# Block attention and a two-layer network: an order planned at build time, and seven products in place of eight for 32 of 36 tiles

## The chip, the cores and the metric

The kernel runs on one core of a Trainium2 chip. A core has five engines, each with its own queue of instructions that it runs strictly in order: TensorE (PE in the profile) multiplies matrices, VectorE (DVE) and ScalarE (ACT) work on elements, GpSimd (POOL) copies and issues loads, SyncE (SP) issues transfers. Sixteen DMA engines move data. Engines wait for each other through semaphores. TensorE writes into PSUM, eight banks of 2 KB per partition; the other data lie in SBUF, 128 partitions.

The metric is the time of one execution on the device, in microseconds (us). The kernel before has a median of 286.15 us over 3 runs (285.52 to 287.26).

## The reference

Inputs are q, k and v of 8 batches, 8 heads, 576 positions and 64 elements per head, and two weights. Attention is computed inside chunks of 64 positions only, so each chunk sees itself alone; its result is the input of a two-layer network without biases.

```python
scores = scale * np.matmul(q_c, k_c.transpose(0, 1, 2, 4, 3))    # chunks of 64
scores = scores - np.max(scores, axis=-1, keepdims=True)
attn = np.exp(scores)
attn = attn / (np.sum(attn, axis=-1, keepdims=True) + 1e-09)
out = np.matmul(attn, v_c)
...
x = np.ascontiguousarray(attn_out.transpose(0, 2, 1, 3)).reshape(B * S, H * D)
...
h = x @ w_in                      # 4608 x 512 by 512 x 2048
g = np.maximum(0.01 * h, h)
return (g @ w_out).astype(np.float32)     # 4608 x 2048 by 2048 x 512
```

Inputs and output are float32; the kernel multiplies in float16.

## The kernel before, in words

The 4608 tokens are 36 tiles of 128 tokens, two chunks each.

**Attention of a tile**, by stages that each stand in one function (lines 539 to 675). q and k are loaded as float16 by GpSimd (`load_qk`, line 64; float32 in memory, cast on the way). For tiles 0 to 8 TensorE transposes them into PSUM (`stage_tq`, `stage_tk`) and VectorE or ScalarE copies them out (`stage_q`, `stage_k`); from tile 9 on SP does it by DMA transposes (`stage_t`, line 563: QT and KT), and GpSimd spreads QT into QZ, a block-diagonal form (`stage_p`, line 571). Then: 8 products into the bank Sp (`stage_s`, line 578), the maximum mx and the shift sh on VectorE, the exponential ex on ScalarE, the sum z, its reciprocal zi and the norm en on VectorE, a transpose into et (`stage_e` and `stage_c` on TensorE and VectorE up to tile 8, `stage_d`, line 642, by SP's DMA from tile 9 on), 8 products with v into xp (`stage_v`, line 651), and ScalarE's copy into xT (`stage_a`, line 669), a ring of 1536 tokens. v lies in VB, two batches, loaded by `load_v`. The buffers for q and k hold 9 tiles.

**The first layer** takes blocks of tokens (`BLOCKS`, line 45: six of 128, three of 256, six of 512). `mm1` fills one bank hT with 512 columns: 4 hidden groups of 128 tokens, 2 of 256 or one of 512, by `SUB`. ScalarE applies the leaky ReLU into gT (`act1`).

**The second layer** is plain for the first 9 blocks (`PLAIN`, 12 tiles): `mm2`, 16 products of 512 columns for each 128 tokens into oP. For the other six blocks (24 tiles) it is Strassen's scheme: the block of g and w_out are cut into 2 x 2 parts, and 7 products take the place of 8 (`product`, line 273, banks ma, mb, mc). It needs sums of weight parts (`weight_form`, WF, five once), sums of parts of g (`form`, S1, S2, S5 and two in place, five a block) and combinations of results (`evict` on ScalarE, `combine` on VectorE, `piece` in the last block), before SP stores them.

**What sets the order.** Emission order is each engine's order. The loads go out first, by the string `LOADS` (line 118). The first five tiles follow a list written by hand (`FRONT`, line 724), in which `i12` stands for 12 idle products that keep TensorE at work while it waits. Then a loop (line 756) makes one round for each tile: Sp and the softmax of one tile, the q and k of another, xp of a third, and six units of the two layers, which `pick` takes from a list by costs kept in `T` and `when`. Loads run 7 tiles ahead of the round, transposes of q and k 3 ahead. A tile's xp comes two rounds after its Sp.

Of the kernel before, what the change touches and what calls it, by code (L numbers as in the profile page):

```python
# [12 lines left out]
AXL = mybir.AxisListType  # L13


@with_exitstack
def kernel(
# [31 lines left out]
    HB, HM = NFC // 2, d_model // 2  # L49

# [3 lines left out]

# [7 lines left out]
    qk: dict[int, tuple[bass.AP, bass.AP]] = {}  # L62

    def load_qk(u):

        both = []
        for name, src in (("q_in", q), ("k_in", k)):
            t = sbp.tile([128, H, D], FP16, name=name, tag=name, bufs=NIN)
            r0, r1 = u * G, (u + 1) * G
            cut = min(-(-r0 // S) * S, r1) if r0 % S else r1  # L70
            for a, z in ((r0, cut), (cut, r1)):
                if a < z:
                    nc.gpsimd.dma_start(  # L73
                        out=t[a - r0:z - r0],
                        in_=src[a // S, :, a % S:a % S + z - a, :].rearrange("h p d -> p h d"),
                    )
            both.append(t)
        qk[u] = tuple(both)

    def load_v(b):  # L80
        for m in range(2):
            nc.gpsimd.dma_start(  # L82
                out=VB[b % NVB][m * CH:(m + 1) * CH, :, :, m * CH:(m + 1) * CH].rearrange("p h c d -> p (h c) d"),
                in_=v[b, m * H // 2:(m + 1) * H // 2].rearrange("h (c j) d -> j (h c) d", j=CH),
            )

    def load_w_in(f0, f1):
        for m in range(2):
# [5 lines left out]
    def load_w_in_quarter(a):  # L94
        load_w_in(512 * a, 512 * a + 512)

    def load_w_out_quarter(a):
        load_w_out(4 * a, 4 * a + 4)

    def load_w_out(f0, f1):  # L100
        nc.gpsimd.dma_start(
            out=w_outT[:, f0:f1, :],
            in_=moe_w_out[f0 * 128:f1 * 128, :].rearrange("(fb p) m -> p fb m", p=128),
        )

    first = []
    for eng, name, src in ((nc.sync, "q_f", q), (nc.scalar, "k_f", k)):
        t = sbp.tile([128, H, D], FP32, name=name, tag=name, bufs=1)
        eng.dma_start(out=t, in_=src[0, :, 0:G, :].rearrange("h p d -> p h d"))
        first.append(t)  # L110
    one = sbp.tile([128, 1], FP16, name="one")
    nc.vector.memset(one, 0.0)
    nc.scalar.activation(out=one, in_=one, func=AFT.Exp, bias=0.0, scale=1.0)
    zeros = sbp.tile([128, 1], FP16, name="zeros")
    nc.vector.memset(zeros, 0.0)
    qk[0] = tuple(sbp.tile([128, H, D], FP16, name=n, tag=n, bufs=NIN) for n in ("q_in", "k_in"))

    LOADS = (
        "g1 v0 g2 Q0 Q1 g3 Q2 Q3 g4 P0 P1 P2 P3 g5 v1 g6 g7 g8 "
    )  # L120
    LOADERS = {"g": load_qk, "v": load_v, "Q": load_w_in_quarter, "P": load_w_out_quarter}
    ident = sbp.tile([128, 128], FP16, name="ident")
    for n, what in enumerate(LOADS.split()):
        LOADERS[what[0]](int(what[1:]))
        if n == 0:
            make_identity(nc, ident)

    gT: dict[int, bass.AP] = {}
    GT: dict[int, tuple[int, bass.AP]] = {}

    def tile_of(j):

        return 0 if j < 4 else 1 if j < 6 else 2 if j < 8 else j - 5

    START = [sum(BLOCKS[:j]) for j in range(len(BLOCKS))]
    mm_n = {"n": 0, "of": 4}

    def mm_tile(shape, name):

        i = mm_n["n"] % mm_n["of"]  # L140
        mm_n["n"] += 1
        return psp.tile(shape, FP32, name=name, tag=f"mm{i}", bufs=1)


    T = {"pe": 0.0, "dve": 0.0, "act": 0.0}

    def on(engine, us, after=0.0):
        T[engine] = max(T[engine], after) + us
        return T[engine]

    UNIT = 0.87
    when: dict[tuple, float] = {}

    HT: dict[tuple[int, int, int], bass.AP] = {}
    parts: dict[tuple[int, int], int] = {}
    oP: dict[tuple[int, int], bass.AP] = {}
    made: dict[int, int] = {}
    read = {"tokens": 0}

    def sub(j):  # L160
        return SUB.get(j, BLOCKS[j])

    def mm1(j, a, h=0):
        tb = sub(j)
        r0 = START[j] + h * tb
        nf = 512 // tb
        hT = mm_tile([128, nf, tb], "hT")
        for i in range(nf):
            fc = nf * a + i
            for t in range(NT):  # L170
                nc.tensor.matmul(  # L171
                    out=hT[:, i, :],
                    lhsT=w_inT[:, t, fc * 128:(fc + 1) * 128],
                    rhs=xT[:, t, r0 % RING:r0 % RING + tb],
                    start=(t == 0),
                    stop=(t == NT - 1),
                )
        on("pe", UNIT)
        HT[j, a, h] = hT
        made[j] = made.get(j, 0) + 1  # L180
        if made[j] == NFC * BLOCKS[j] // 512:
            read["tokens"] = START[j] + BLOCKS[j]

    def act1(j, a, h=0):
        tb = sub(j)
        nf = 512 // tb
        n = tile_of(j)
        if n not in GT:
            GT[n] = START[j], sbp.tile([128, NFC, 512], FP16, name="gT", tag="gT", bufs=2)
        gT[j] = GT[n][1][:, :, START[j] - GT[n][0]:START[j] - GT[n][0] + BLOCKS[j]]  # L190
        nc.scalar.activation(  # L191
            out=gT[j][:, nf * a:nf * a + nf, h * tb:h * tb + tb], in_=HT.pop((j, a, h)),
            func=AFT.Prelu, bias=0.0, scale=1.0, alpha=0.01,
        )
        when["gT", j] = on("act", 0.62, T["pe"] + 0.2)

    def mm2(j, ti, part):
        n = parts.get((j, ti), 0)
        if n == 0:
            oP[j, ti] = mm_tile([128, d_model], "oP")  # L200
        o = oP[j, ti]
        for fc in range(part * 4, part * 4 + 4):
            nc.tensor.matmul(  # L203
                out=o,
                lhsT=gT[j][:, fc, ti * 128:(ti + 1) * 128],
                rhs=w_outT[:, fc, :],
                start=(n == 0 and fc == part * 4),
                stop=(n == NFC // 4 - 1 and fc == part * 4 + 3),
            )
        on("pe", UNIT)  # L210
        parts[j, ti] = n + 1

    def store(j, ti):
# [3 lines left out]
        r0 = START[j] + ti * 128  # L217
        nc.sync.dma_start(out=out[r0:r0 + 128, :], in_=osb)

# [249 lines left out]
    def pick():  # L469
# [5 lines left out]
        if not can:  # L475
            return None
# [347 lines left out]
```

## Time and profile before

| | us |
|---|---|
| median of 3 runs | 286.15 |
| fastest, slowest run | 285.52, 287.26 |
| span of the profiled execution | 285.7 |
| TensorE busy | 275.5 |
| VectorE busy | 193.8 |
| ScalarE busy | 149.4 |
| GpSimd busy | 128.1 |

The profile gives the span, from the first instruction to the last, as the profiled execution's time; it is 0.45 us below the median of the runs, which were timed apart from it. A busy time is the union of an engine's instructions. A line such as "L298 PE MATMUL mb<-WF,gT ... x8" names the source line, the engine, what is written and what is read, and how many instructions are merged; the numbers ahead are the start and the duration in us. A unit's last products are drawn past the next unit's start, because matrix products are pipelined: the pace is read from one start to the next. In brackets stands the idle time ahead of a group and what ended it. "DMA to landing" is the time from the issue of a transfer to its semaphore.

### The profile page before, as it was taken

How to read it: one execution, taken by the hardware profiler on the slowest of the kernel's cores; microseconds unless marked ns; L12 is line 12 of the kernel's file. 1: busy time of each engine (PE TensorE's matmuls, PEld its weight loads, DVE VectorE, ACT ScalarE, POOL GpSimd, SP SyncE). 2: the span in 40 equal slices, each digit the busy share in tenths (PEclk: the TensorE clock that was granted, in tenths of full speed). 3: DMA queues.
4: the chain of work that ended last, by engine and by line, in shares of the span. 5: the costliest groups of instructions: out<-in, count | busy, mean ns of one | idle time of the engine just before them, and what ended most of it. 6: DMA issues, size and time to landing. Idle time of an engine off the chain costs nothing.

```text
span 285.7 us, 7255 instructions
## 1 busy us (share of the span) xinstructions
PE 275.5 (96%) x3012; PEld 226.3 (79%) x3012; DVE 193.8 (68%) x322; ACT 149.4 (52%) x264; POOL 128.1 (45%) x166
## 2 busy tenths in 40 slices
PE   4979999999999999999999999999999999999995
PEld 4969855877949585899989899998999998666784
DVE  6987515666687776557888888888888840820392
ACT  6347733655738374777356546554565554535320
POOL 8846646876585647657538495332410000000000
PEclk9999999999999999999999999999999999999999
DMA  9999999999999999999999999999714301200213
GB/s 131 170 189 179 192 165 195 143 180 162 175 147 173 158 156 184 162 157 134 155 154 158 139 188 197 153 136 249 114 30 112 93 2 73 76 0 0 110 59 129
DMA packets 165825, 39.14 MB, mean 137 GB/s; under 512 B 156832, under 2 KB 161440, under 8 KB 165792
## 3 DMA queue, kind: packets, MB, share of 16 engines
q0 software_dynamic: 114336, 18.09, 91.5%
q1 hardware_dynamic: 50416, 20.33, 42.8%
q8 instruction: 23, 0.38, 0.5%
q10 hardware_dynamic: 1040, 0.26, 0.4%
q14 instruction: 10, 0.08, 0.1%
HBM read 36.70 MB, written 9.44 MB: 161 GB/s over the span
## 4 chain that ended last, share of the span: by engine, by line
PE 84%; DMA 6%; DVE 5%; ACT 2%; issue 1%; POOL 1%; ACTq 0%; POOLq 0%
PE hT L171 40%; PE oP L203 15%; PE mb L298 10%; PE mc L298 7%; PE ma L298 6%; DMA k_in<-in_k_dram 4%; PE xp L657 3%; PE Sp L583 2%; DMA VB<-in_v_dram 2%; DVE S L263 2%; ACT ex L605 1%; ACT gT L191 1%; DVE en L622 1%; PE kp L547 1%; DVE sh L598 0%
## 5 line engine op out<-in xcount | busy, mean ns | idle before, releaser
L171 PE MATMUL hT<-xT,w_inT 128*128 128x256 f16 (+2 forms) x1344 | 143.4, 257 | 1.9 <-DMA w_inT<-in_moe_w_in_dram 0.9
L171 PEld LDWEIGHTS <-w_inT 128*128 128x128 f16 x1344 | 107.6, 98 | 15.6 <-issue 2.6
L191 ACT ACTIVATE gT<-hT 128x512 f16<-128x512 f32 x144 | 85.5, 595 | 54.5 <-PE hT L171 53.3
L576 POOL COPY QZ<-QT 64x512 f16<-64x512 f16 x54 | 36.5, 676 | 53.0 <-DMA QT<-q_in 34.1
L203 PE MATMUL oP<-w_outT,gT 128*128 128x512 f16 x192 | 44.9, 379 | 0.0
L298 PEld LDWEIGHTS <-gT 128*128 128x128 f16 x384 | 37.5, 98 | 6.2
L605 ACT ACTIVATE ex<-sh 128x512 f16<-128x512 f32 x36 | 22.6, 627 | 33.7 <-DVE sh L598 33.6
L73 POOL DMA_DIRECT2D k_in<-in_k_dram x39 | 32.9, 845 | 15.9 <-DVE z L612 4.1
L612 DVE TENSOR_REDUCE z<-ex 128x8 f32<-128x512 f16 x36 | 24.7, 685 | 21.1 <-ACT ex L605 20.9
L593 DVE TENSOR_REDUCE mx<-Sp 128x8 f32<-128x512 f32 x36 | 24.7, 686 | 18.1 <-PE Sp L583 18.0
L73 POOL DMA_DIRECT2D q_in<-in_q_dram x39 | 33.2, 851 | 7.0 <-DMA w_outT<-in_moe_w_out_dram 2.4
L298 PEld LDWEIGHTS <-S 128*128 128x128 f16 x288 | 28.1, 98 | 5.0 <-DVE S L263 0.5
L203 PEld LDWEIGHTS <-gT 128*128 128x128 f16 x192 | 17.6, 98 | 17.7
L622 DVE TENSOR_TENSOR en<-ex,zi 128x512 f16<-128x512 f16 x36 | 27.2, 757 | 1.2
L673 ACT ACTIVATE xT<-xp 128x512 f16<-128x512 f32 x36 | 21.3, 592 | 9.4 <-PE xp L657 9.4
L598 DVE TENSOR_TENSOR sh<-Sp,mx 128x512 f32<-128x512 f32 x36 | 24.9, 691 | 1.2
L298 PE MATMUL mb<-WF,gT 128*128 128x256 f16 x192 | 24.6, 273 | 0.0
L263 DVE TENSOR_TENSOR S<-gT 128x2048 f16<-128x2048 f16 x18 | 22.3, 1278 | 1.5 <-ACT gT L191 1.5
L82 POOL DMA_DIRECT2D VB<-in_v_dram x16 | 18.5, 1161 | 0.0
L215 ACT ACTIVATE osb<-oP 128x512 f32<-128x512 f32 x12 | 7.2, 597 | 18.4 <-PE oP L203 18.4
L657 PEld LDWEIGHTS <-VB 128*128 128x128 f16 x288 | 13.1, 98 | 3.1 <-issue 0.6
L583 PEld LDWEIGHTS <-QZ 128*128 128x128 f16 x288 | 13.2, 99 | 2.2 <-issue 0.3
(57 smaller groups left out, 233.2 us busy)
## 6 DMA issues: line engine op xcount, KB each, us to landing
out_dram<-osb SPq DMA_DIRECT2D x10, 512.0 KB, 3.5
VB<-in_v_dram POOLq DMA_DIRECT2D x16, 288.0 KB, 13.2
q_in<-in_q_dram POOLq DMA_DIRECT2D x31, 128.0 KB, 13.1
k_in<-in_k_dram POOLq DMA_DIRECT2D x31, 128.0 KB, 13.6
out_dram<-osb SPq DMA_DIRECT2D x14, 256.0 KB, 6.8
w_inT<-in_moe_w_in_dram POOLq DMA_DIRECT2D x8, 256.0 KB, 9.7
w_outT<-in_moe_w_out_dram POOLq DMA_DIRECT2D x4, 512.0 KB, 9.9
q_in<-in_q_dram POOLq DMA_DIRECT2D x8, 64.0 KB, 9.1
```

The costliest lines, as they stand in the source:

```text
L73: nc.gpsimd.dma_start(out=t[a - r0:z - r0], in_=src[a // S, :, a % S:a % S + z - a, :].rearrange("h p d -> p h d"),)
L171: nc.tensor.matmul(out=hT[:, i, :], lhsT=w_inT[:, t, fc * 128:(fc + 1) * 128], rhs=xT[:, t, r0 % RING:r0 % RING + tb], start=(t == 0), sto ...
L191: nc.scalar.activation(out=gT[j][:, nf * a:nf * a + nf, h * tb:h * tb + tb], in_=HT.pop((j, a, h)), func=AFT.Prelu, bias=0.0, scale=1.0, a ...
L203: nc.tensor.matmul(out=o, lhsT=gT[j][:, fc, ti * 128:(ti + 1) * 128], rhs=w_outT[:, fc, :], start=(n == 0 and fc == part * 4), stop=(n == ...
L263: nc.vector.tensor_tensor(out=to, in0=of, in1=by, op=op)
L298: nc.tensor.matmul(out=BANK[bank][:, p, :] if j < LAST else ENDS[bank, p], lhsT=lhs[:, fc, p * 128:(p + 1) * 128], rhs=rhs[:, fc, :], star ...
L576: nc.gpsimd.tensor_copy(out=QZ[u % NQZ][part, :, :, s, :], in_=qt[part])
L593: nc.vector.tensor_reduce(out=MX[u], in_=SP[u], axis=AXL.X, op=ALU.max)
L598: nc.vector.tensor_tensor(out=SH[u], in0=SP.pop(u), in1=MX.pop(u).unsqueeze(2).to_broadcast((128, 8, CH)), op=ALU.subtract)
L605: nc.scalar.activation(out=E[u], in_=SH.pop(u), func=AFT.Exp, bias=0.0, scale=SCL)
L612: nc.vector.tensor_reduce(out=z, in_=E[u], axis=AXL.X, op=ALU.add)
L622: nc.vector.tensor_tensor(out=E[u], in0=ex, in1=ZI.pop(u).unsqueeze(2).to_broadcast((128, 8, CH)), op=ALU.mult)
```

## The change

The loop, the hand-written list and the picking are replaced by a planner that runs while the program is built. Every step is a task with an engine (or a choice of engines), a duration, the tasks it depends on, a place in the wished order (`pos`), and for PSUM a bank that it takes and the tasks that free it. The planner keeps a clock for each engine and a model of the DMA queues, takes the task that can begin first, among those within `SLACK` the one with the smallest `pos`, and emits it. The resulting order is fixed in the program; nothing of the plan is present when it runs.

```diff
+class Planner:
+    LAG = 0.035
...
+    def advance(self, to):
+        for k, r in self.heads().items():
+            self.queues[k][0][1] -= r * (to - self.now)
+        self.now = to
+        for q in self.queues.values():
+            while q and q[0][1] <= 1e-9:
+                n, _, _, _, kind = q.pop(0)
+                lat = 1.5 if kind != "turn" else 3.2 if self.queues.get("sw") else 0.4
+                self.landings.append((to + lat, n))
...
-    BLOCKS = [128] * 6 + [256] * 3 + [512] * 6
-    PLAIN = 9
-    SUB = {7: 128, 9: 256, 10: 256, 11: 256, 12: 256, 13: 256}
+    BLOCKS = [128]*4+[256]*4+[512]*6
+    PLAIN = 4
+    SUBS = {}
+    LEAD = 3.49
+    LOADS = 'g1 v0.0 i v0.1 g2 Q0 Q2 g3 Q1 Q3 P0 g4 P2 P1 g5 g6 P3 v1.0 v1.1 g7 g8'
...
-        "g1 v0 g2 Q0 Q1 g3 Q2 Q3 g4 P0 P1 P2 P3 g5 v1 g6 g7 g8 "
...
+    plan = Planner(
+        {"mm": ["qp", "kp", "mm0", "mm1", "mm2", "mm3"], "Sp": ["Sp"], "ox": ["ox"]}, SLACK
+    )
...
+    def att(u, step=0.0):
+        return (first_pos(u - LEAD) + ATT + 0.001 * step if u >= 4 else -10 + u + 0.01 * step) + TWEAK.get((u, step), 0.0)
...
+            add(("e", u), {"SP": (1.3, 1.3)}, turn_e_dma(u), [("n", u), ("v", u - 4)], dma=("turn", 0.77, 0.024), pos=p(u, -5))
...
+        add(("v", u), {"PE": (0.233, 0.40)}, values(u), vd, pos=p(u, 12), bank="ox", frees=[("a", u)])
...
+    def fill(since, at):
+        tags = [(x, k) for k, x in plan.banks["mm"].items() if x is not None and x <= since]
+        n = int((at - since) * FILLS / 0.056) - 1
+        if since < FILL and tags and n > 1:
+            to = psum([128, 4, 128], FP32, "idle", min(tags)[1])
+            for i in range(n):
+                nc.tensor.matmul(out=to[:, i % 4, :], lhsT=ones, rhs=ones, start=True, stop=True)
...
+    plan.gap = fill
+    plan.run()
```

What differs in the work itself:

- Second layer: plain for 4 tiles instead of 12; seven products for four blocks of 256 tokens (4 to 7) and the six of 512. For a block of 256 the sums and results have half the width.
- First layer: units of 128 columns for 4 tiles instead of 8, all others of 256 columns; the 512-column units of the last block are gone.
- Loads: in `LOADS` g is a tile's q and k, v a batch's v, Q and P quarters of w_in and w_out, i the identity matrix. In the built order the first v stands behind tile 2; Q2 ahead of Q1, P0 ahead of tile 4, tile 6 and P3 ahead of the second v. Later loads stand where the planner put them, between GpSimd's copies.
- Idle products read a tile of ones instead of the identity, and are put where the plan leaves TensorE idle before 24 us: 175 instead of 120.
- The banks for seven-product results, first-layer units and transposes come from one pool of six.
- Up to tile 8 the copies of q and k go to VectorE or ScalarE, as the planner finds them free.
- In the built order, the last block's products begin before those of the block ahead of it are done: five units stand between the last first-layer unit and the first product that reads S2.

On TensorE the built order has 144 first-layer units (16 of 128 columns, 128 of 256), 16 plain second-layer units and 112 of the seven products; before it was 32, 96 and 16 (of 512), 48 and 84. The attention's pieces are the same in number.

More of the change, by code (lines that the diff above doesn't have):

```diff
@@ L80, in load_v @@
-    def load_v(b):
-        for m in range(2):
+    ident = sbp.tile([128, 128], FP16, name="ident")
+    one = sbp.tile([128, 1], FP16, name="one")
+    ones = sbp.tile([128, 128], FP16, name="ones")
+    zeros = sbp.tile([128, 1], FP16, name="zeros")
+    plan = Planner(
+        {"mm": ["qp", "kp", "mm0", "mm1", "mm2", "mm3"], "Sp": ["Sp"], "ox": ["ox"]}, SLACK
+    )
+    add = plan.add
+    copy = {"DVE": (0.40, 0.46), "ACT": (0.52, 0.62), "POOL": (0.61, 0.66)}
+    dve = {"DVE": (0.69, 0.72)}
@@ new lines, with either, block_of, first_pos @@
+    act = {"ACT": (0.53, 0.62)}
+    def either(eng, out, in_):
+        if eng == "ACT":
+            nc.scalar.activation(out=out, in_=in_, func=AFT.Copy, bias=0.0, scale=1.0)
+        elif eng == "DVE":
+            nc.vector.tensor_copy(out=out, in_=in_)
+        else:
+            nc.gpsimd.tensor_copy(out=out, in_=in_)
+    def block_of(tile_n):
+        return next(j for j in range(LAST, -1, -1) if START[j] <= tile_n * 128)
+    def first_pos(tile_n):
+        j = block_of(max(0, min(NU - 1, tile_n)))
+        return j - 1 + (tile_n * 128 - START[j]) / BLOCKS[j]
```

1230 lines of the change are left out of this document (644 added, 586 removed), and 6 rows, old and new, of the table FRONT.

## The prediction

> **What bounds the kernel now.** I read the page from the top: span, engines, slices, the chain that ended last. Then TensorE's waits, the timeline around its first and last products, and at last one tile's way through the engines.
>
> ```profile
> span 285.7 us, 7255 instructions
> PE 275.5 (96%) x3012; PEld 226.3 (79%) x3012; DVE 193.8 (68%) x322; ACT 149.4 (52%) x264; POOL 128.1 (45%) x166
> PE   4979999999999999999999999999999999999995
> DMA  9999999999999999999999999999714301200213
> PE 84%; DMA 6%; DVE 5%; ACT 2%; issue 1%; POOL 1%; ACTq 0%; POOLq 0%
> ```
>
> TensorE is busy in every slice but the first three and the last, and 84% of the chain is its own work. The DMA engines are full for 28 of 40 slices, but do they set the pace? The waits say no: after the start nothing keeps TensorE.
>
> ```profile
> PE idle L681 <- POOL ident masks.py:199: 3.8, 1, 3.8
> PE hT L171 <- DMA w_inT<-in_moe_w_in_dram: 0.9, 2, 0.5
> PE xp L657 <- DVE et L638: 0.5, 1, 0.5
> PE mb L298 <- DVE S L263: 0.2, 1, 0.2
> ```
>
> So the time is what TensorE must do, plus a start set by loads, plus an end. A change is worth what it takes from TensorE's list, less the waits that a new order brings.
>
> **The change part by part.** I call the products that fill one PSUM bank a unit: 16, 8 or 4 products of a first-layer tile hT, 4 of a plain second-layer tile oP, 8 of one of the seven products.
>
> ```profile
> 28.01 1.06 PE L171 MATMUL hT<-xT,w_inT 128*128 128x128 f16 x16
> 28.90 0.39 PE L631 MATMUL tpe<-ident,en 128*128 128x128 f16 x4
> 110.31 0.40 PE L583 MATMUL Sp<-KT,QZ 128*128 128x64 f16 x8
> 110.54 3.62 PE L203 MATMUL oP<-w_outT,gT 128*128 128x512 f16 x16
> 114.00 0.40 PE L657 MATMUL xp<-et,VB 128*128 128x64 f16 x8
> 116.20 3.66 PE L171 MATMUL hT<-xT,w_inT 128*128 128x256 f16 x32
> 119.69 0.40 PE L657 MATMUL xp<-et,VB 128*128 128x64 f16 x8
> 125.40 0.40 PE L657 MATMUL xp<-et,VB 128*128 128x64 f16 x8
> ```
>
> From start to next start, a 128-column unit of hT costs 0.89 us; four plain units 3.46, so 0.865 each; four 256-column units 3.49, so 0.873 each, which I take for a seven-product unit too (8 products of the same 256 columns). An attention piece Sp costs 0.23.
>
> *Second layer.* Plain tiles go from 12 to 4: 8 x 4 = 32 plain units leave, 27.7 us. Eight tiles by seven products are four blocks of 7 units: 28 units come, 24.4 us. Gain 3.2 us.
>
> *First layer.* Sixteen 128-column units and the last block's sixteen 512-column units (0.865, 4 products of 512 like a plain one) become 32 of 256 columns: 14.2 + 13.8 out, 27.9 in. Gain 0.1.
>
> *The end.* Before, the last block's seven products stand alone at the end, and S2 is late:
>
> ```profile
> 269.77 1.91 PE L298 MATMUL ma<-WF,gT 128*128 128x256 f16 x16
> 270.60 3.50 DVE L263 TENSOR_TENSOR S<-gT 128x2048 f16<-128x2048 f16 x3 [0.74 <-ACT gT L191]
> 271.88 1.92 PE L298 MATMUL mb<-w_outT,S 128*128 128x256 f16 x16 [0.20 <-DVE S L263]
> ```
>
> Sixteen products take 1.75 and would end at 271.52; the next start at 271.88: 0.36 lost. The new order holds five other units between the last hT and the first product that reads S2, 4.4 us, which hides this. Gain 0.4. What follows the last product is the same sum and store.
>
> *The front.* First-layer units cannot start before their weights and tiles:
>
> ```profile
> 14.07 1.00 PE L681 MATMUL idle<-ident 128*128 128x128 f16 x15
> 16.71 1.05 PE L171 MATMUL hT<-xT,w_inT 128*128 128x128 f16 x16 [0.45 <-DMA w_inT<-in_moe_w_in_dram]
> 22.34 0.40 PE L547 MATMUL kp<-ident,k_in 128*128 128x128 f16 x4 [0.17 <-DMA k_in<-in_k_dram]
> 22.57 1.06 PE L171 MATMUL hT<-xT,w_inT 128*128 128x128 f16 x16
> ```
>
> The same loads precede tile 3's k in both queues (only v of batch 0 and tile 2 change places, and two w_in quarters), so I keep 22.57 for the fourth unit. The new order has one more xp before it: gain 0.2. The idle products, 120 before and 175 after, fill waits and cost nothing while these loads are late; without that cover one run of 16 would cost 1.1 us (15 took 1.00). Loads behind this point: v of batch 1 now stands behind tile 6's q and k.
>
> ```profile
> 46.90 0.89 POOL L73 DMA_DIRECT2D q_in<-in_q_dram  x1
> L82 POOL DMA_DIRECT2D VB<-in_v_dram x2: 1182/1184/1187, 29.3 to 30.5; - x2
> DMA to landing us min/median/max: 13.6/14.3/15.0
> q_in<-in_q_dram POOLq DMA_DIRECT2D x1, 128.0 KB, 7.2
> k_in<-in_k_dram POOLq DMA_DIRECT2D x1, 128.0 KB, 7.1
> ```
>
> Its second half landed at 30.5 + 15.0 = 45.5. A q load and the k load behind it, issued 0.89 later, landed 7.2 and 7.1 after their issues, so two loads move it by about 1.8, to 47.3. In the new order tile 4's xp, which needs it, comes 13 hT units, 12 oP units and 14 attention pieces after 22.57: 11.6 + 10.4 + 3.2, at 47.8. Just in time; nothing taken, 1 us if late.
>
> *The new order in the middle.* This is the price. In the old loop each tile's xp stands two rounds after its Sp: 110.31 to 125.40 above, 15.1 us. What must fit between:
>
> ```profile
> 110.75 0.69 DVE L593 TENSOR_REDUCE mx<-Sp 128x8 f32<-128x512 f32 x1 [0.87 <-PE Sp L583]
> 112.92 0.69 DVE L612 TENSOR_REDUCE z<-ex 128x8 f32<-128x512 f16 x1 [0.76 <-ACT ex L605]
> 114.08 0.69 DVE L622 TENSOR_TENSOR en<-ex,zi 128x512 f16<-128x512 f16 x1
> 115.27 1.39 SPq L644 DMA_TRANSPOSE et<-en  x1
> DMA to landing us min/median/max: 2.4/7.5/9.5
> QT<-q_in SPq DMA_TRANSPOSE x1, 6.2
> et<-en SPq DMA_TRANSPOSE x1, 2.4
> ```
>
> From Sp to the issue of et's transpose is 115.27 - 110.31 = 5.0; the transpose then takes 7.5 (median of 27), 6.2 between 190 and 194 us, where the loads run out, 2.4 between 200 and 205, where none are left. The planner reckons 1.3 + 0.8 + 3.2 = 5.3 with loads in flight (its own constants, below every loaded row), and places each xp as soon as that has passed. Counting units in the new order, Sp to xp has room for 10.5 us at tiles 18 and 26, 11.4 at 15, 12.3 at 11 and 14, 13 to 16 at most others up to 29. A shortfall is TensorE idle: everything behind xp on its queue waits. From tile 30 on the room is 7.2 to 7.5, which the unloaded 2.4 fits; it holds if the loads are done by 200 us, as before. With 5.0 + 5.3 nothing is short. With 5.0 + 6.2 = 11.2: 0.7 at 18 and at 26, 1.4. With 12.5: 0.2 + 0.2 + 0.9 + 2.0 + 2.0 = 5.3 (a shift between a tile's Sp and its xp is counted once). I take 1.0, between the first two: in the new order a tile's three transposes come every 6.7 us instead of 5.7, so fewer overlap. That is the weakest choice here.
>
> [...]
>
> *POOL and SP.* On POOL the loads now stand between the copies of q: k of tile 13 is behind the copies of tiles 9 and 10 and waits for their transposes. Tile 13's Sp is 26 us of units behind tile 8's, so this is covered. On SP the stores of results stand between transposes, as before.
>
> *VectorE.* Sums for 256-token blocks (128x1024) are not in the trace. Half of the 128x2048 row is a lower end, the whole an upper.
>
> ```profile
> L263 DVE TENSOR_TENSOR S<-gT 128x2048 f16<-128x2048 f16 x18 | 22.3, 1278 | 1.5 <-ACT gT L191 1.5
> L387 DVE TENSOR_TENSOR osb<-mc,td 128x256 f32<-128x256 f32 x2 | 0.8, 424 | 2.0 <-PE mc L298 2.0
> L340 DVE TENSOR_TENSOR osb<-mc,td 128x512 f32<-128x512 f32 x5 | 3.4, 685 | 11.5 <-PE mc L298 11.5
> 160.00:215.00 55.00, 55.00 (x622) 49.54 (x620) 48.07 (x77) 30.03 (x56) 24.00 (x30) 1.00 1.45 150
> ```
>
> Halving the combines leaves 0.62 of the time, so a half form may be 0.78; bounds 0.64 and 1.28, I take 0.70. From tile 8's Sp to tile 17's the new order gives TensorE 52 units and 18 pieces, 49.5 us, and VectorE nine tiles' softmax, 20 such sums and 16 combines of 0.42. The softmax of a tile is 3.3 by its six instructions from 110.75 to 114.77 without the 0.76 that it waits there for the exponential: 29.7 + 14.0 + 6.7 = 50.4. VectorE is full there. But it was 87% busy from 160 to 215 with no wait on TensorE, and its spare time lies on both sides; I take 0, and 0 to 3 for the range (at 0.78 it is 2.5 over; at 1.28 12).
>
> **Sum**, on the profiled execution's span: 285.7 - 3.2 - 0.1 - 0.4 - 0.2 + 1.0 = 282.8. The median of the runs, 286.15, is 0.45 above that span, so 283.2.
>
> **The rivals.**
> 1. *VectorE becomes the bound* between 60 and 110 us. For: the sum of 50.4 against 49.5. Against: 55 us at 87% without a wait. Price 2.5 more than forecast: 285.7.
> 2. *The plan's latencies hold* and xp never waits: 282.2. For: two thirds of tiles 9 to 29 have 13 us and more. Against: no loaded row is as short as 5.3.
> 3. *Transposes keep the loaded median* of 7.5: waits of 5.3 instead of 1.0, 287.5, no change to speak of.
> 4. *Slower:* the same place, but with sums and combines of the new blocks standing in VectorE's queue between a tile's maximum and its norm (in the new order two sums and a combine at tile 11, 1.7 us), or transposes near 8.5. At Sp to xp of 13.5 the shortfalls are 0.4 at tile 9, 1.2 at 11 and 14, 0.9 at 15, 3.0 at 18, 0.3 at 21, 3.0 at 26: 10.0, time 292.2. It decides from 12.9 us on, where the waits reach 6.8 and the time passes 289.0.
> 5. *The change does not do what it says:* fewer second-layer products but the old time, because a plan can't be kept in queues that run in order. This is 3 and 4 together.
>
> **How the numbers follow.** One per cent of the median, about what a measurement of this kernel can tell from no change, is 2.9 us. Forecast and rival 2 (282 to 284.5): 0.48, of which 0.44 lies below 283.3. Rival 1 0.12, rival 3 0.15, rival 4 0.25. So faster 0.44, same 0.31, slower 0.25. The range begins at 281.0, 1.2 under rival 2 for a front quicker by one run of idle products, and ends at 290.0, inside rival 4, with 0.2 left out.
>
> **What would show it.** Right: 16 oP and 112 seven-product units at 0.865 and 0.873; no wait on the sums at the end; the fourth hT unit near 22.6; TensorE waits on et of about 1 us in all, at tiles 18 and 26. Wrong: TensorE waiting for transposes or VectorE by several us between 60 and 190; a dense stretch that begins more than 1 us before or after 22.6; a half form far from 0.70; et landing 7 us or more after its issue.

## The result, and the profile after

The changed kernel takes 305.26 us (median of 4 runs, 302.78 to 306.24), the kernel before 285.9 us beside it (285.52 to 287.26). The ratio is 1.065, with a 95% interval of 1.060 to 1.071: slower, where the prediction said 283.2 us and nothing above 290.0. The profiled execution is the longest of the four: it took 306.24 us, 1.8 us more than its span.

The page of the changed kernel, from the span to the chain that ended last:

```profile
span 304.4 us, 7481 instructions
...
PE 282.9 (93%) x3099; PEld 245.8 (81%) x3099; DVE 203.0 (67%) x354; ACT 156.7 (51%) x277; POOL 131.7 (43%) x166
...
PE   8899999969969998999799979998699999999995
...
PEclk9999999997988999999799998999999999999999
...
PE 64%; DMA 26%; POOL 7%; issue 1%; DVE 0%; ACT 0%; SPq 0%; POOLq 0%
```

TensorE's own work was 84% of the chain before; now it is 64%, and transfers are 26%. TensorE's row has holes between the 9th and the 29th slice, and a row that was full before has some too: the granted clock (PEclk). Who TensorE waited for, in the view of its waits (us in total, times, longest):

```profile
PE xp L525 <- DMA et<-en: 11.5, 7, 2.5
PE Sp L451 <- DMA KT<-k_in: 2.3, 1, 2.3
PE Sp L451 <- POOL QZ L231: 1.1, 2, 0.7
...
PE Sp L451 <- DVE gT L682: 0.2, 1, 0.2
```

These four are all of its waits behind 60 us: 15.1 us, and 14.5 of it for DMA transposes, the 0.7 us for one QZ among them, a copy of QT that began as QT landed. The other wait for QZ, 0.3 us at 144.27, is GpSimd's own: QT had landed at 135.69, and the copy stood behind load issues until 142.05. The timeline of TensorE around three of them (start, duration, line, what; in brackets the idle time ahead and what ended it):

```profile
65.48 0.39 PE L500 MATMUL tpe<-ident,en 128*128 128x128 f16 x4
68.22 0.39 PE L451 MATMUL Sp<-KT,QZ 128*128 128x64 f16 x8 [2.35 <-DMA KT<-k_in]
68.44 3.11 PE L608 MATMUL hT<-xT,w_inT 128*128 128x256 f16 x16
...
81.28 1.91 PE L608 MATMUL hT<-xT,w_inT 128*128 128x256 f16 x16
83.02 0.40 PE L451 MATMUL Sp<-KT,QZ 128*128 128x64 f16 x8
...
88.47 0.39 PE L525 MATMUL xp<-et,VB 128*128 128x64 f16 x8 [2.43 <-DMA et<-en]
88.70 2.90 PE L608 MATMUL hT<-xT,w_inT 128*128 128x256 f16 x16
...
220.09 0.39 PE L525 MATMUL xp<-et,VB 128*128 128x64 f16 x8 [2.52 <-DMA et<-en]
```

There is a second price. Sixteen products that take 1.91 us at 81.28 take 3.11 us behind the first wait and 2.90 behind the second. The view by windows shows why (stretch, length, busy us of each engine with its instructions, then the granted clock):

```profile
69.00:70.70 1.70, 1.70 (x10) 1.21 (x8) 0.23 (x1) 0.60 (x1) 0.00 (x0) 0.50 2.19 124
70.70:72.40 1.70, 1.70 (x16) 1.33 (x14) 0.00 (x0) 0.81 (x2) 0.12 (x1) 0.51 1.98 171
72.40:73.40 1.00, 1.00 (x12) 0.89 (x10) 0.18 (x1) 0.28 (x1) 1.00 (x1) 1.00 2.60 136
```

Soon after the wait TensorE gets half its clock for 3.4 us. The same record of the clock has 0.50 from 69.0, 89.5, 147.5 and 181.6 us, 3.4 us each time: 13.6 us at half speed, 6.8 us lost. This is the account of one execution; in the shortest of the four runs (span 301.0 us) the mean granted clock is 0.994, against 0.978 here.

So the difference of the spans, 18.7 us, is accounted for: 15.1 of waits and 6.8 of clock, less the 3.9 us that the prediction took off (3.2, 0.1, 0.4 and 0.2), plus 0.6 us by which the dense part begins later (23.14 instead of 22.57). That is 18.6. The waits and the clock come from the same trace, so this shows that nothing large is missing, not what made the waits; that is for the experiments.

### The profile page after: what moved, and what is told of

The parts are those of the page before. It is cut to its first block, busy times and chain, and to the rows that moved or that the text cites. A ratio compares the mean times of both kernels' runs of the same rounds, so it can differ in the third digit from the quotient of the medians.

```text
span 304.4 us, 7481 instructions
## 1 busy us (share of the span) xinstructions
PE 282.9 (93%) x3099; PEld 245.8 (81%) x3099; DVE 203.0 (67%) x354; ACT 156.7 (51%) x277; POOL 131.7 (43%) x166
## 4 chain that ended last, share of the span: by engine, by line
PE 64%; DMA 26%; POOL 7%; issue 1%; DVE 0%; ACT 0%; SPq 0%; POOLq 0%
PE hT L608 30%; DMA et<-en 13%; PE mb L705 10%; PE mc L705 7%; PE ma L705 7%; DMA QT<-q_in 6%; PE oP L633 4%; DMA q_in<-in_q_dram 4%; DMA KT<-k_in 3%; PE xp L525 2%; PE Sp L451 2%; POOL k_in L268 2%; POOL q_in L268 2%; POOL VB L276 1%; POOL QZ L231 1%
## 5 line engine op out<-in xcount | busy, mean ns | idle before, releaser
L608 PE MATMUL hT<-xT,w_inT 128*128 128x256 f16 (+1 forms) x1280 | 147.8, 266 | 0.1
L608 PEld LDWEIGHTS <-w_inT 128*128 128x128 f16 x1280 | 114.9, 99 | 13.6 <-PE idle L877 0.2
L231 POOL COPY QZ<-QT 64x512 f16<-64x512 f16 x54 | 40.3, 745 | 77.3 <-DMA QT<-q_in 38.3
L705 PEld LDWEIGHTS <-gT 128*128 128x128 f16 x512 | 49.2, 98 | 5.5
L705 PEld LDWEIGHTS <-S 128*128 128x128 f16 x384 | 38.3, 102 | 5.5
L481 DVE TENSOR_REDUCE z<-ex 128x8 f32<-128x512 f16 x36 | 24.6, 683 | 19.3 <-ACT ex L475 19.1
L682 DVE TENSOR_TENSOR S<-gT 128x2048 f16<-128x2048 f16 (+1 forms) x30 | 30.7, 1033 | 8.9 <-ACT gT L622 8.7
L705 PE MATMUL mb<-WF,gT 128*128 128x256 f16 x256 | 33.2, 273 | 0.0
L535 ACT ACTIVATE xT<-xp 128x512 f16<-128x512 f32 x36 | 21.4, 594 | 18.8 <-PE xp L525 18.6
L525 PE MATMUL xp<-et,VB 128*128 128x64 f16 x288 | 14.5, 194 | 11.5 <-DMA et<-en 11.5
L525 PEld LDWEIGHTS <-VB 128*128 128x128 f16 x288 | 13.2, 99 | 14.1 <-issue 12.3
L276 POOL DMA_DIRECT2D VB<-in_v_dram x16 | 18.5, 1165 | 11.2 <-PE xp L525 11.1
L682 DVE TENSOR_TENSOR gT<-gT 128x2048 f16<-128x2048 f16 (+1 forms) x20 | 20.8, 1046 | 0.0
L451 PE MATMUL Sp<-KT,QZ 128*128 128x64 f16 x288 | 14.3, 193 | 4.8 <-DMA KT<-k_in 2.3
```

The source lines that it names most:

```text
L231: nc.gpsimd.tensor_copy(out=out, in_=in_)
L451: nc.tensor.matmul(out=Sp[:, i, :], lhsT=qz[:, 2 * m + g, e, :, :], rhs=kt[:, 2 * m + g, e, :], start=True, stop=True)
L481: nc.vector.tensor_reduce(out=z, in_=st["ex", u], axis=AXL.X, op=ALU.add)
L525: nc.tensor.matmul(out=xp[:, t, e, :], lhsT=VB[b % NVB][:, t, c, :], rhs=et[:, t // 2, e, t % 2, :], start=True, stop=True,)
L608: nc.tensor.matmul(out=hT[:, i, :], lhsT=w_inT[:, t, fc * 128:(fc + 1) * 128], rhs=xT[:, t, r0 % RING:r0 % RING + tb], start=(t == 0), sto ...
L682: nc.vector.tensor_tensor(out=to, in0=of, in1=by, op=op)
```

## The experiments

Theory A: every long wait is a DMA transpose that lands later than the plan allows, and the plan leaves no room behind the planned landing. Rivals: B, the queues of the other engines can't keep the order, whatever the allowance; C, the new blocks' sums and combines on VectorE make the waits; D and E, on the clock.

### The allowance raised, and the loads taken away

**Allowance 7.5 us instead of 5.3.**

```diff
-                lat = 1.5 if kind != "turn" else 3.2 if self.queues.get("sw") else 0.4
+                lat = 1.5 if kind != "turn" else 5.4 if self.queues.get("sw") else 0.4
```

> The planner's allowance for a transpose while loads are in flight raised by 2.2 us, from 5.3 us in all to 7.5 us, the loaded median of the kernel before; all else as in the changed kernel. The order is planned anew. Theory A (every long wait of TensorE comes from transposes that land later than the plan allows, with no room behind the planned landing): the waits on et, KT and QT shrink from 15 us to under 3 us, the granted clock stays at 1.00, time 283 to 287 us. Rival B (the order can't be kept by the queues of VectorE, SP and POOL, whatever the allowance): waits of 8 us and more stay, time above 293 us.

Measured: 290.48 us (288.39 to 292.49), ratio 1.015 (1.010 to 1.020). Fifteen of the 19 us are gone by one number. In the profiled execution (span 290.7 us) the waits on transposes are 4.9 us (2.1 for a KT, 2.4 for an et, 0.4 for QZ); two of them are followed by the half clock, 3.4 us lost; without both the span would be 282.4. This execution is the longest of four; the shortest took 288.39 us. Between A and B: the mechanism of A, with the allowance still short (the et of the 2.4 us took 10.2 us, where 7.5 were allowed).

**The same order without loads.**

```diff
+            if u >= 13:
+                qk[name, u] = qk[name, u - NIN]
+                return
...
+            if b >= NVB:
+                return
```

> The order of the changed kernel unchanged, instruction for instruction, but the loads of q and k from tile 13 on and of v from batch 2 on are left out (old data is used again, so the result is not the reference's). Theory A (landings under load): et lands within 2.4 to 3 us from about 75 us on, the waits behind tile 10's are gone, the granted clock dips at most twice, before 95 us; time 284 to 290 us. Rival B (the chain from Sp to the issue of et on VectorE and SP is the cause, 9.4 to 12 us at tiles 10, 20, 21, 23, 28): waits of 5 us and more stay behind tile 10's, time 293 us or more.

Measured: 282.72 us (282.41 to 283.2), ratio 0.988 (0.986 to 0.990): better than A had it, and B falls. Span and engines on the page of this run:

```profile
span 280.7 us, 7380 instructions
...
PE 274.1 (98%) x3099; PEld 242.4 (86%) x3099; DVE 201.9 (72%) x354; ACT 156.4 (56%) x277; POOL 77.0 (27%) x102
```

and the last row of the view of its tile et, all 27 transposes:

```profile
DMA to landing us min/median/max: 2.4/2.4/4.4
```

Not one wait on a transpose of 0.15 us or more is left, and the clock is full as long as TensorE works. The order itself, instruction for instruction, is faster than the kernel before as soon as transposes land in 2.4 us. (GpSimd's work also falls with the loads; but only 0.3 us of TensorE's waits led there other than through QT.) In the changed kernel the same row reads:

```profile
DMA to landing us min/median/max: 2.4/5.8/8.9
```

### Blocks and order taken apart

**The planner with the blocks of before.**

```diff
-    BLOCKS = [128]*4+[256]*4+[512]*6
-    PLAIN = 4
+    BLOCKS = [128]*6+[256]*3+[512]*6
+    PLAIN = 9
```

> The changed kernel with the blocks of the kernel before (six of 128 tokens, three of 256, twelve plain tiles); order, loads and the planner's constants as changed. Theory A (the planned order is the cause): TensorE's list is about 3 us longer than in the changed kernel and the waits stay, time 303 to 312 us. Rival C (the sums and combines of the four new seven-product blocks crowd VectorE and make the waits): time 286 to 293 us.

Measured: 313.66 us (310.61 to 315.69), ratio 1.093; TensorE waits 19.1 us for et, up to 5.3 at once. The four new blocks are innocent: without them the plan waits more, also more than A had expected. C falls for the planned order.

**The new blocks in the order of before.** The same `BLOCKS` and `PLAIN` as changed, in the old kernel, `SUB` to match (256 columns for blocks 8 to 12), and

```diff
-        if 11 <= it < 16:
-            weight_form(it - 11)
+        if it == 6:
+            weight_form(3)
+            weight_form(4)
...
+        "B0.3 f0 tq5 f1 O0 tk5 q5.0 B1.1 k5 q5.1 B1.2 B1.3 B2.0 f2 O1 "
```

> The kernel before with its hand-written order and its loads, and only the new blocks: four of 128 tokens, four of 256, six of 512, of which the first four are plain; the sums of the weights are moved to the front, because the first seven-product block comes sooner. Theory A (the products are worth the 3.2 us that the unit counts give, and the planned order took the time): 282 to 285 us, no waits on et. Rival C (the four new blocks cost more on VectorE or in PSUM banks than they save on TensorE): 286 to 295 us, with TensorE waiting for sums, combines or banks between 45 and 110 us.

Measured: 308.47 us (307.63 to 310.34), ratio 1.077. Theory A's number was wrong by more than 23 us. The view of TensorE's waits there, in which S and gT are the sums:

```profile
PE ma L298 <- DVE S L263: 5.0, 2, 2.5
...
PE mb L298 <- DVE gT L263: 2.7, 1, 2.7
PE hT L171 <- ACT xT L673: 2.3, 3, 0.9
PE mb L298 <- DVE osb L343: 2.1, 1, 2.1
PE mc L298 <- DVE S L263: 1.7, 2, 0.9
```

They lie between 53 and 132 us, five half-clock stretches with them. In the old loop, at this place, the sums come too late for the products, which is the mechanism of C, at more than its price; the fewer products don't pay there. This placing of the weights' sums is one of many, so it shows that the products need another order, not that no old order could carry them.

### The chain from Sp to et

The prediction had 5.0 us from a tile's Sp to the issue of et's transpose. Over tiles 9 to 29 the changed kernel has a median of 7.7, between 4.5 and 12.0, read from the timelines of TensorE and SP. Three runs asked what makes it long.

**VectorE's sums left out** (the products read gT itself):

```diff
-            nc.vector.tensor_tensor(out=to, in0=of, in1=by, op=op)
-            SF[j, m] = to
+            SF[j, m] = of
```

> The order of the changed kernel unchanged, but VectorE's 50 sums S and gT of the seven products (52 us of VectorE's time) are left out and the products read gT itself, so the result is not the reference's; loads and transposes stay. Theory G (the wait is landing plus a chain from Sp to the issue of et that VectorE's sums lengthen, median 7.7 us where 5.0 was reckoned): Sp to issue falls to 5 to 6 us, the waits on et fall from 11.5 us to under 5 us, time 288 to 296 us. Rival H (the landings alone decide): waits of 9 us and more, 299 to 306 us.

Measured: 306.27 us (304.47 to 307.56), ratio 1.069. VectorE is 159.3 us busy instead of 203.0, the chain's median is 8.0, TensorE waits 14.5 us for et. Theory G falls; the load of the sums on VectorE is not the cause.

**The combines left out:**

```diff
+            elif m in (2, 1, 5):
+                return
+            elif m == 6:
+                nc.vector.memset(osb_of(j, 1)[:, ix, HM:], 0.0)
+            elif m == 7:
+                nc.vector.memset(osb_of(j, 0)[:, ix, :HM], 0.0)
```

> The order of the changed kernel unchanged, but VectorE's combines of the seven products are left out: three of five of a block are dropped, the two that write results are replaced by constant writes that wait for no product, so the result is not the reference's. The sums stay. Theory I (the softmax steps of a tile stand in VectorE's queue behind combines, which wait for products that TensorE reaches later; this makes the 7.7 us from Sp to the issue of et where 5.0 was reckoned): Sp to issue falls to 5 to 6.5 us at the median, waits on et under 7 us, time 288 to 298 us. Rival H (the landings decide whatever the chain): waits of 9 us and more, 299 to 306 us.

Measured: 300.77 us (298.66 to 302.61), ratio 1.050; the chain's median 7.0, waits on et 10.8 us. Theory I at most in part.

**Both left out:**

> As the run without combines, with the 50 sums left out as well, so that VectorE has nothing but the softmax and its copies between a tile's maximum and its norm. Theory I: Sp to issue 4.5 to 5 us at the median (the shortest of the changed kernel is 4.5); with landings of 6 to 8 us the room of 10.5 to 16 us is then short by 2 to 5 us in all; 285 to 291 us. Rival H: waits of 9 us and more, 297 us or more.

Measured: 299.42 us (297.17 to 303.2), ratio 1.043. In the profiled execution, the longest of the four, the chain's median is 7.5 and TensorE waits 12.3 us for et. Theory I falls as well. The waits of all three runs are within what H had, but in none of them did the chain get short, so what a short chain would be worth is not shown. What else holds the softmax of a tile up is shown, for tile 12, by the changed kernel's own timelines of ScalarE and, behind the dots, of VectorE:

```profile
85.20 0.60 ACT L622 ACTIVATE gT<-hT 128x512 f16<-128x512 f32 x1 [1.38 <-PE hT L608]
88.90 0.60 ACT L535 ACTIVATE xT<-xp 128x512 f16<-128x512 f32 x1 [3.10 <-PE xp L525]
89.93 0.60 ACT L622 ACTIVATE gT<-hT 128x512 f16<-128x512 f32 x1 [0.43 <-PE hT L608]
90.42 0.62 ACT L475 ACTIVATE ex<-sh 128x512 f16<-128x512 f32 x1
...
86.42 0.68 DVE L466 TENSOR_TENSOR sh<-Sp,mx 128x512 f32<-128x512 f32 x1
...
91.08 0.69 DVE L481 TENSOR_REDUCE z<-ex 128x8 f32<-128x512 f16 x1 [3.38 <-ACT ex L475]
```

The shift of tile 12 is done at 87.10. Its exponential stands in ScalarE's queue behind the copy of tile 10's xp, and that xp waited until 88.47 for its et. So a late et of one tile makes the softmax of the tile after next late, and with it the next et: it was issued 10.7 us after its Sp. VectorE hands lateness on in the same way, in its timeline at tile 10:

```profile
73.22 0.42 DVE L737 TENSOR_TENSOR td<-td,mb 128x256 f32<-128x256 f32 x1 [3.99 <-PE mb L705]
73.56 0.68 DVE L460 TENSOR_REDUCE mx<-Sp 128x8 f32<-128x512 f32 x1
```

The maximum of Sp, there since 68.6, stands behind a combine that waits for products behind TensorE's own wait at 68.22.

But most of the 7.7 is no lateness: the run without loads, which has no long wait, keeps a median of 7.4, and the plan's own times have 7.7 from Sp to the issue as well (4.6 to 10.4), and place each xp of tiles 9 to 29 only 0.0 to 0.8 us behind the planned landing. For the seven tiles where TensorE waited on et (10, 15, 19, 21, 23, 27, 28) et landed 16.2 us later in sum, counted from issue, than the plan's 5.3 to 5.5, and the chains up to the issue were 6.5 us longer than planned.

### Which transposes

**The allowance raised for et alone, to 9.6 us.**

```diff
+                lat = 1.5 if kind != "turn" else (7.5 if n[0] == "e" else 3.2) if self.queues.get("sw") else 0.4
```

> The changed kernel with the planner's allowance raised for the transpose of et alone, by 4.3 us to 9.6 us in all; QT and KT keep 5.3 us. Theory A, with et as the main part (11.5 us of the 15 us of waits) and QT and KT as the rest: waits on et under 1.5 us, one or two waits on KT or QZ of about 2 us each stay, 286 to 290 us. Rival F (the waits on QT and KT, early in a chain, are what makes the et of later tiles late): waits on et of 4 us and more stay, above 292 us.

Measured: 288.72 us (288.25 to 289.07), ratio 1.009 (1.006 to 1.012): as A had it. No wait on et of 0.15 us or more is left; what stays in the view of its waits, behind those of the front, is

```profile
PE Sp L451 <- DMA KT<-k_in: 1.6, 1, 1.6
...
PE mc L705 <- DVE S L682: 0.9, 1, 0.9
PE Sp L451 <- POOL QZ L231: 0.7, 1, 0.7
```

The et of most tiles was late in its own right, not through QT and KT; F falls.

### The clock

**Idle products in the waits.**

```diff
+    def warm_up(to, n):
+        for i in range(n):
+            nc.tensor.matmul(out=to[:, 2 * (i % 4):2 * (i % 4) + 2, :], lhsT=ones, rhs=ones, start=True, stop=True)
...
+            warm_up(Sp, 24 if u == 10 else 0)
...
+            warm_up(xp.rearrange("p t e c -> p (t e) c"), 24 if u in (10, 19, 23, 28) else 0)
```

> The changed kernel with 24 idle products (1.3 us of TensorE) put ahead of the scores of tile 10 and of the values of tiles 10, 19, 23 and 28, where TensorE waited 1.9 to 2.5 us; the waits have room for them. Theory D (the granted clock falls to 0.50 for 3.4 us after a stretch with 1.9 us or more of idle, and this costs 6.8 us of its own): the clock stays at 1.00 and the time falls by 4 to 7 us, to 299 to 302 us. Rival E (time lost to the clock is only moved: later waits grow by as much): 304 to 307 us, whether the clock falls or not.

Measured: 309.93 us, but the four runs lie far apart (303.39, 309.24, 310.62 and 313.16). The profile is of the one of 310.62 us: the two stretches of half clock at tile 10 are gone (full clock up to 118.9 us), but later waits are longer: 3.3, 2.6 and 3.9 us, each with its half clock. Only in the run of 303.39 us is the mean granted clock 1.00; it is 1.9 us under the changed kernel's median, where D had 4 to 7. One run does not decide between D and E: that the 6.8 us come back when the clock is held is not shown.

### Room enough

**Allowance 8.6 us, tile 9 on TensorE** (`3.2` to `6.5`, `UD = 9` to `10`):

> The changed kernel with the allowance for a loaded transpose raised by 3.3 us to 8.6 us for QT, KT and et, and tile 9 transposed on TensorE like the tiles before it, so that the first DMA transposes come one tile later. The run without loads took 2.7 us more than its plan's end; this plan ends 1.2 us later than that one's. Theory A: no wait over 1 us between 60 and 200 us, granted clock 1.00, 283 to 285 us, faster than the kernel before by about 0.7%. Rival B (other queues hold the order up): 287 us or more.

Measured: 289.49 us (287.31 to 291.54), ratio 1.011. In a profiled run of 287.31 us, the shortest, TensorE still waits 3.4 us for et. A miss of 4 us and more. The longest of these waits, 2.0 us, is for an et that took 10.6 us.

**Allowance 9.6 us** (`7.5`, `UD = 10`, `A_LEAD = 0.1`):

> As the one with more room, with the allowance raised by 4.3 us to 9.6 us and the first layer's lead over the second shortened (0.23 to 0.10), which this allowance needs for a dense plan; its plan ends 0.6 us later than that of the one with more room. Theory A: 283.5 to 285.5 us, no wait over 1 us; if the run with more room still waits for late landings by 1 us or more, this one is the faster of the two. Rival B: 287 us or more.

Measured: 286.87 us (285.11 to 289.77), ratio 1.001 (0.998 to 1.004); one wait of 1.8 us. A's time is missed by 1.4 us, but it is the faster of the two.

**The same with the blocks of before:**

> The kernel with most room (9.6 us allowed, second layer by seven products for 32 tiles), with the blocks of the kernel before (24 tiles by seven products). By the counts of units TensorE's list is 3.3 us longer; by its plan 2.1 us. Theory A (the products are worth what they take from TensorE's list once the order has room): 289 to 290.5 us against 286.9 us. Rival C (the new blocks' sums on VectorE give the gain back): 287 us or less.

Measured: 295.52 us (295.06 to 297.58), 8.7 us above the run before it. Theory C falls again, but A's size is off: 5.0 us of waits on et and 3.4 us of half clock come on top of the longer list. The longer of the two waits, 3.6 us, is for an et that took 6.6 us where the planner, in its model of the loads, held them for done and allowed 2.5. So the 8.7 us don't measure the blocks.

**Replanned under long allowances.** With one number changed, the planner's other weights were still those chosen for 5.3 us. Two runs had them chosen anew for the shortest plan: 10.6 us for et and 8.6 for QT and KT, and 10.6 for all three.

```diff
+                lat = 1.5 if kind != "turn" else (8.5 if n[0] == "e" else 6.5) if self.queues.get("sw") else 0.4
+    UD = 10
+    LEAD = 3.15
+    ATT = -0.71
+    FORM = -1.0
...
+    A_LEAD = 0.51
```

> The changed kernel planned with 10.6 us for et's transpose and 8.6 us for those of q and k while loads are in flight, tile 9 transposed on TensorE, and the planner's weights (how far attention leads, when sums are due, single nudges) chosen anew for the shortest plan under these allowances; the plan ends 0.5 us behind that of the changed kernel. Theory A (room behind Sp and behind the transposes is all that was missing): no waits over 1 us, 282.5 to 284.5 us, faster than the kernel before by 0.6 to 1.2%. Rival B (a dense plan with this room still meets late landings or late sums): 285.5 us or more.

Measured: 285.05 us (284.2 to 287.98), ratio 0.997 (0.994 to 1.000), and, a second time,

> The run replanned with 10.6 and 8.6 us a second time, beside fresh runs of the kernel before: 284.5 to 286 us if 285.1 us was no accident of the chip; a ratio to the kernel before under 1.000.

285.98 us (283.93 to 287.77), ratio 0.998 (0.995 to 1.000). Both times are above A's range; the waits on et are 2.8 and 1.6 us.

> As the one before, with 10.6 us for all three transposes and tiles 9 and 10 transposed on TensorE; the plan ends 0.7 us later than that. Theory A: 283 to 285 us. If landings of q and k over 8.6 us matter, this one is the faster; if not, it is slower by its plan, 0.7 us. Rival B: 286 us or more.

Measured: 286.50 us (284.99 to 288.92), ratio 1.001. Of the waits on transposes one is left, for tile 18's et, in the timelines of TensorE and, the middle row, of SP:

```profile
114.84 0.40 PE L451 MATMUL Sp<-KT,QZ 128*128 128x64 f16 x8
...
124.34 1.53 SPq L513 DMA_TRANSPOSE et<-en  x1
...
134.37 0.39 PE L525 MATMUL xp<-et,VB 128*128 128x64 f16 x8 [2.01 <-DMA et<-en]
```

The transpose took 9.9 us, less than the 10.6 allowed; it was issued 9.5 us after Sp, where the plan has 6.5. In both runs replanned here no et took longer than 9.9 us, and their longest waits stand where the chain, not the landing, was later than planned (in the profiled execution of the first, 1.3 us at tile 28: 15.6 us instead of 11.2). In these executions it is late chains that use up the room.

**Two more, with 11.6 us for et.**

> As the one before, but q and k keep 8.6 us; et 11.6 us; the plan's end is the same within 0.1 us. Theory A: 283 to 284.8 us; the waits on et under 1 us, at most one wait on KT or QZ. Rival B: 285 us or more.

Measured: 286.57 us (284.83 to 288.81), ratio 1.001; waits on et 0.6 us, but 2.0 for QZ. The waits are as A had them, the time is B's.

> The changed kernel planned anew with 11.6 us for et's transpose and 9.6 us for those of q and k under load, tile 9 transposed on TensorE, the planner's weights chosen for the shortest plan under these allowances; the plan ends 0.1 us behind that of the run replanned with 10.6 and 8.6 us. Theory A (what is left between that run's 285.1 us and 282.7 us without loads is landings beyond the allowance): the waits on et fall under 1 us, 282.8 to 284.6 us, faster than the kernel before by 0.5% or more. Rival B (what is left isn't room for landings): 285 us or more.

Measured: 293.99 us (292.37 to 298.86), which says nothing on the allowance: in this order the values of tile 17 come ahead of tile 16's, batch 5's v is loaded over batch 3's as soon as tile 17 is done, so tile 16 is computed with other data than the reference's, and TensorE waits 5.0 us for that load.

**Room for all three** (`9.0` for et, `8.0` for QT and KT, the weights chosen anew, `LEAD = 3.11`, `FORM = -0.85`, and each load of v held for all readers of its buffer):

```diff
-                deps += [("v", max(users))]
+                deps += [("v", x) for x in users]
```

> The changed kernel planned anew with 11.1 us for et's transpose and 10.1 us for those of q and k under load, tile 9 transposed on TensorE, each load of v held until all tiles that read its buffer are done; the plan ends 0.07 us behind that of the run replanned with 10.6 and 8.6 us. Theory A (what is left above 282.7 us is landings beyond the allowance, of all three transposes): waits on et, KT and QZ together under 1.5 us, 283 to 285 us. Rival B (what is left is not mended by room): 285.5 us or more.

Measured: 284.67 us (283.76 to 285.32), beside 286.47 us for the kernel before; ratio 0.994 (0.991 to 0.996). This beats both kernels, the one before by 0.6%, and is as A had it. Span, engines and clock on its page:

```profile
span 282.0 us, 7495 instructions
...
PE 275.2 (98%) x3111; PEld 243.0 (86%) x3111; DVE 203.8 (72%) x356; ACT 157.2 (56%) x279; POOL 130.6 (46%) x164
...
PEclk9999999999999999999999999999999999999999
```

and the landing of et:

```profile
DMA to landing us min/median/max: 2.4/6.4/8.8
```

No wait on a transpose is left. Landings are as late as in the changed kernel and the chain is as long (median 7.5), but Sp to xp has a median of 19 us instead of the 13.2 us that the changed kernel's units leave. Here no et took longer than 8.8 us, 2.3 under its allowance, and no chain was later than planned by more than 1.5 us. A median of 19 us from Sp to xp is in both runs replanned above too, so room alone does not tell this order from those. Why its chains stay closer to the plan is open: each allowance was tried with one order, and this is the best of five.

## Why the prediction was wrong

**What held.** TensorE's list: the units still take 0.87 us (81.28 to 83.02 is two), and the run without loads, whose span of 280.7 us lies under the 281.8 that the sum gives without its 1.0 for waits, shows the list to be as short as forecast. The front, nearly: the fourth first-layer unit at 23.14, against 22.57 (tile 3's k landed at 22.34, as before at 22.30, but its q at 21.52 instead of 20.61, and a unit and an xp stood between); no wait for v of batch 1. The end, in the timeline of TensorE: five units, from the first of these rows to the second, hide S2,

```profile
286.24 1.04 PE L705 MATMUL mc<-WF,gT 128*128 128x256 f16 x8
...
290.60 1.04 PE L705 MATMUL mb<-w_outT,S 128*128 128x256 f16 x8
```

with no idle time between them and S2 ready at 288.3. The half form, in the groups by line with shapes apart:

```profile
L682 DVE TENSOR_TENSOR S<-gT 128x1024 f16<-128x1024 f16 x12 | 8.3, 707 | 2.1 <-ACT gT L622 2.1
```

0.71 us for the 0.70 taken; the two in-place sums take 0.78. Rival 1, VectorE as the bound, is refuted by the run without sums.

**The step that failed** is the 1.0 us in "The new order in the middle". Three things in it were wrong.

First, the chain. "From Sp to the issue of et's transpose is 115.27 - 110.31 = 5.0" was one tile of the kernel before, and a short one: its median over tiles 9 to 29 is 5.8, and in the new order 7.7. The rooms of 10.5 to 16 us were then read as if all beyond 5.0 were spare. They were not: the prediction itself says that the planner places each xp as soon as 5.3 us have passed, and that holds behind each tile's own chain. Where the room is 16 us, the chain is 10. No tile had anything to spare, so the late places were not 18 and 26, the narrowest rooms (there the chains are 4.5 and 4.6, and et landed in 2.9 and 3.5), but 10, 15, 19, 21, 23, 27 and 28.

Second, the landing. The transposes did land sooner in the middle (median 5.8 instead of 7.5; over tiles 9 to 29 alone 6.4 instead of 7.7), though that the wider spacing did it is not shown. But a sum of waits is set by the late ones, and they reach 8.9 us. In the run without loads, with the same order, they do not: 2.4 us at the median, 4.4 at most. The prediction gave its rival with the loaded median 0.15.

Neither error alone makes waits of this size. An estimate from the plan's times and the trace, by the prediction's own count of shortfalls over tiles 9 to 29: its 1.4 us (5.0 and 6.2 for all) becomes 5.4 with each tile's planned chain and 6.2, 4.4 with 5.0 and each tile's measured landing, and 12.9 with the planned chains and the measured landings. Measured for et: 11.5.

Third, what a wait sets off. Rival 4 had the right mechanism, late et in an order with no room, and gave 292.2 us as its price. It lacked the half clock (6.8 us) and the lateness that ScalarE's and VectorE's queues pass on. That SP and GpSimd cost nothing was wrong too, by the 3.4 us of KT and QZ. SP's part of it, in the timeline:

```profile
53.23 1.48 SPq L440 DMA_TRANSPOSE QT<-q_in  x1
58.71 0.34 SPq L649 DMA_DIRECT2D out_dram<-osb  x1
59.23 2.60 SPq L440 DMA_TRANSPOSE KT<-k_in  x1
```

KT of tile 10, whose k had landed at 54.9, stands behind the store of a result, 4 us in which SP issues nothing, and lands at 68.1. The old loop issues these transposes three rounds ahead of their Sp, so that a store between them cost it no wait of TensorE; "as before" overlooked that.

With 15.1 and 6.8 us in place of 1.0, and 0.6 for the front, the prediction's sum gives a span of 304.3 us, where 304.4 was measured.

## What to carry to other kernels

A planned order is as good as its longest constants: a planner that packs work against a latency turns every excess of that latency into idle time, so give it the late end of what the trace shows under load and some more for a chain that comes late, and then let it choose the order anew. When room is counted in a new order, take each item's own chain from that order, not one duration for all, and ask how much of the room the plan has already spent. And an engine that waits in order hands its lateness to the engines whose queues hold its results, so price a wait with what it sets off.

## What the runs showed of the hardware

In the changed kernel the granted clock is 0.50 from 69.0, 89.5, 147.5 and 181.6 us; the distances, 20.5, 58.0 and 34.1, are 6, 17 and 10 times 3.41, and each stretch lasts 3.41. In the 3.4 us ahead of these stretches TensorE was idle for 2.35, 2.43, 2.49 and 1.93 us, with the clock at 1.00; the last of these is one wait of 1.94 us (ended at 181.16). The longest wait of all, 2.52 us, was followed by no half clock. Counted on from 181.6 by 11 times 3.41 stands 219.1, which cuts this wait into 1.5 and 1.0, in the view by windows:

```profile
217.50:219.10 1.60, 0.07 (x1) 0.00 (x0) 0.00 (x0) 0.60 (x1) 0.00 (x0) 1.00 1.61 63
219.10:220.10 1.00, 0.01 (x1) 0.01 (x1) 0.00 (x0) 0.00 (x0) 0.00 (x0) 1.00 1.03 115
220.10:221.80 1.70, 1.70 (x28) 1.57 (x28) 1.01 (x2) 0.60 (x1) 0.90 (x2) 1.00 1.42 115
```

In the 3.4 us ahead of 219.1 and in the 3.4 us behind it TensorE has no other idle time, and the granted clock is 1.00 in both. What sets the half clock off is not shown; in this execution the length of a wait alone doesn't tell it, since 1.94 us was followed by half clock and 2.52 was not.

The DMA transpose of et (128 x 512) landed 2.4 us after its issue in the run without loads (median of 27, 4.4 at most); beside loads it took 2.6 to 8.9 us (et of tiles 9 to 29 in the changed kernel), and up to 10.2 us in the run without sums and 10.6 in the one with sums and combines left out.
